# A fused attention and mixing kernel: first batch ordered by hand, constants moved to VectorE, later batches' reorder copies queued behind mixing, zero matmuls during the loads

## The chip, the cores and the metric

The kernel runs on one core of a Trainium2 chip. The metric is the device time of one execution in microseconds (us), the median of several executions on the chip. Single executions of the kernel before took 213.1 to 214.9 us. Runs are called fast or slow by their granted TensorE clock and time.

## The reference, cut to what matters

```python
B, H, S, D = 4, 8, 768, 64          # attention; then x is [4, 768, 512]
scores = q @ k.T / 8 + bias          # kept: 96 latest positions and 8 global ones
x = softmax(scores) @ v              # heads side by side
theta = x @ w_theta
zr, zi = x * cos(theta), x * sin(theta)
u = x + w_tok_r @ zr + w_tok_i @ zi  # over the 768 positions ("mixing")
out = u + relu(u @ w_ch)
```

The work is in bf16. For each batch: reorder and transpose q and k (four pairs of heads), scores, exponentials, values, transpose x, theta, mixing, the channel product.

## The kernel before: the parts that matter

The attention of batch b+1 is woven into the mixing of batch b, so that TensorE always has work. Batch 0 has no earlier batch and runs alone while the loads of everything else are still coming in. A scheduler decides the order of the instructions on each engine; the profile below shows what this means for VectorE, where a ready instruction stands behind a waiting one.

```python
def prep(b, p):                       # reorder a head pair (VectorE), transpose (TensorE)
    qkn = att.tile([T, NT, 2, 2, D], BF, name="qkn", bufs=3)
    for i_ in range(2):               # q, then k: each waits for its load
        nc.vector.tensor_copy(out=qkn[:, :, i_]..., in_=qk[:, i_, 2 * p:2 * p + 2])   # L175
    ...
        nc.tensor.transpose(ps[:, t_, :], qkn[:, t_, i_]..., ident)                    # L182

def values(b, p, hh): ...
    nc.vector.reciprocal(rec, po4[:, :, :, D:D + 1])                                   # L268
    nc.vector.tensor_mul(xv, po4[:, :, :, 0:D], rec...)      # x_sb, normalised          L270

def xtrans(b, p, copy): ...           # xT <- transposes of x_sb                         L275, L276

load_w(); load_all(1)
for p in range(NP):
    prep(0, p)
    for c in range(NT // 2):
        if p < NP - 1: scores(0, p, c)
globals_(0)
for p in range(NP):
    vglob(0, p); values(0, p, 0)
    if p < NT // 2: scores(0, NP - 1, p)
    values(0, p, 1)
    if p:
        trans_w(p - 1, nc.scalar.copy); xtrans(0, p - 1, nc.scalar.copy)
xtrans(0, NP - 1, nc.scalar.copy)
for b in range(B):                    # theta(b), then mixing woven with prep and attention of b+1
    ...
    pre = [(1536, lambda p=p: prep(nxt, p)) for p in range(NP)] if nxt else []
```

(Cuts are marked with "...".)

The softmax here doesn't subtract the row's maximum and nothing guards it: scores larger than these inputs give would overflow.

## Time and profile before

| | before |
|---|---|
| time, median of 3 | 213.73 us |
| span of the profile | 211.4 us |
| end of batch 0's last xT copy (theta can run in full) | 46.41 us |
| from there to the end | 164.96 us |

From the page of the kernel before: the busy tenths of TensorE and VectorE and the granted TensorE clock, in 40 slices of 5.3 us each.

```profile
PE   0586695388999999999999999999999999999971
DVE  3686352335698588657967667578666675652431
PEclk9999999579999999999999999999999999999997
```

TensorE (PE) is saturated from about 50 us on (nine tenths or more in every slice from 53 to 201 us). Before that it is not, and in the seventh and eighth slices (32 to 42 us) it is busy for only five and three tenths of the time. The VectorE (DVE) timeline around that point shows why. The columns are start, busy time, engine, source line, operation, output<-inputs; in brackets, the idle time before it and what ended it.

```profile
33.54 0.23 DVE L268 RECIPROCAL rec<-pb 128x12 f32<-128x12 f32 x1 [0.18 <-PE pb L264]
39.37 0.36 DVE L175 COPY qkn<-qk 128x768 bf16<-128x768 bf16 x1 [5.59 <-DMA qk<-in_q_dram]
39.64 0.95 DVE L270 TENSOR_TENSOR x_sb<-pb,rec 128x768 bf16<-128x768 f32 x1
40.51 0.62 DVE L175 COPY qkn<-qk 128x768 bf16<-128x768 bf16 x2
43.23 0.63 DVE L175 COPY qkn<-qk 128x768 bf16<-128x768 bf16 x2 [2.10 <-DMA qk<-in_k_dram]
43.77 0.23 DVE L268 RECIPROCAL rec<-pb 128x12 f32<-128x12 f32 x1
44.03 0.97 DVE L270 TENSOR_TENSOR x_sb<-pb,rec 128x768 bf16<-128x768 f32 x1
```

The reciprocal of pair 2 is done at 33.77 us and its multiplication could follow at once. Between the two stands a reorder copy of batch 1, which nobody needs yet and whose load lands at 39.37 us.

The TensorE timeline of the same kernel: six transposes of x_sb before 31 us, six of the weights after it, and the first instruction after the stall.

```profile
30.40 0.81 PE L275 MATMUL ps<-ident,x_sb 128*128 128x128 bf16 x6
31.11 0.50 PE L159 MATMUL ps<-ident,w_nat 128*128 128x128 bf16 x6
...
40.65 0.29 PE L275 MATMUL ps<-ident,x_sb 128*128 128x128 bf16 x1 [5.70 <-DVE x_sb L270]
```

Six transposes of the same shape take 0.81 us and then 0.50 us: from one to the next it is about 107 ns and then 55 ns. The array ran at half clock before 31 us: five transposes at 42.56 us, where the clock record has half clock, take 0.72 us, the same 107 ns from one to the next. The PEclk row shows a 9 there all the same (no clock record covers that time; the first begins at 31.06 us). TensorE then waits 5.70 us for the stalled multiplication.

### The profile page before, as it was taken

The numbers are of one execution on the slowest core, as the hardware profiler recorded it, in microseconds if no ns is written. First come the engines' busy times: TensorE is split into PE (matmuls) and PEld (weight loads), VectorE is DVE, ScalarE is ACT, GpSimd is POOL, SyncE is SP. The second block draws the span as 40 slices with busy tenths as digits, with TensorE's granted clock in tenths as the row PEclk, the third lists the DMA queues.
The fourth block names the chain that finished last, engine by engine and source line by source line (L and its number), as shares of the span: only waits on it lengthen the run. The fifth ranks groups of instructions, "written<-read, shape, count | busy, mean of one in ns | idle before, by whom it ended". The sixth has DMA issues, their size and how long they took to land.

```text
span 211.4 us, 4121 instructions
## 1 busy us (share of the span) xinstructions
PE 182.5 (86%) x1726; PEld 100.0 (47%) x1752; DVE 129.5 (61%) x268; ACT 119.4 (56%) x178; POOL 31.2 (15%) x46
## 2 busy tenths in 40 slices
PE   0586695388999999999999999999999999999971
PEld 0453484343464566645535555455354565344420
DVE  3686352335698588657967667578666675652431
ACT  2549859059459554269695652696956525912110
POOL 8992474040030000030000000000000000000000
PEclk9999999579999999999999999999999999999997
DMA  5999999999999611099011100110111011102121
GB/s 75 167 160 179 210 204 205 201 150 197 181 162 185 122 53 50 3 104 144 3 50 50 54 24 29 50 50 3 50 53 50 3 50 54 50 0 99 50 99 50
DMA packets 39329, 19.39 MB, mean 92 GB/s; under 512 B 25488, under 2 KB 36240, under 8 KB 39312
## 3 DMA queue, kind: packets, MB, share of 16 engines
q0 software_dynamic: 35856, 12.85, 61.5%
q1 hardware_dynamic: 3456, 6.29, 8.0%
q8 instruction: 13, 0.21, 0.4%
q14 instruction: 4, 0.03, 0.0%
HBM read 25.69 MB, written 6.29 MB: 151 GB/s over the span
## 4 chain that ended last, share of the span: by engine, by line
PE 66%; DMA 12%; DVE 9%; POOL 6%; issue 3%; ACT 2%; POOLq 0%; ACTq 0%
PE ps L305 28%; PE ps L325 10%; PE pb L290 7%; DMA qk<-in_k_dram 7%; PE pb L264 6%; DMA w_nat<-in_moe_w_tok_r_dram 5%; PE pb L222 4%; PE ps L316 3%; PE ps L182 3%; PE ps L275 2%; DVE zri L297 2%; POOL qk L72 2%; POOL vn L78 1%; DVE qT L187 1%; DVE o_sb L328 1%
## 5 line engine op out<-in xcount | busy, mean ns | idle before, releaser
L305 PE MATMUL ps<-zri,w_tokT_148 128*128 128x512 bf16 x141 | 53.2, 379 | 1.0 <-issue 0.2
L305 PE MATMUL ps<-zri,w_tokT_147 128*128 128x512 bf16 x128 | 48.4, 381 | 1.9 <-DVE zri L297 1.8
L318 ACT COPY uT<-ps 128x512 bf16<-128x512 bf16 x24 | 14.2, 590 | 37.0 <-PE ps L316 37.0
L328 DVE SCALAR_TENSOR_TENSOR o_sb<-ps,u 128x512 f32<-128x512 f32 x24 | 16.5, 689 | 25.4 <-PE ps L325 25.1
L325 PE MATMUL ps<-w_ch_bf,uT 128*128 128x512 bf16 x91 | 24.1, 380 | 1.2 <-ACT uT L318 0.7
L290 PE MATMUL pb<-w_theta_bf,xT 128*128 128x512 bf16 x94 | 24.2, 385 | 0.7 <-ACT xT L276 0.7
L182 PE MATMUL ps<-ident,qkn 128*128 128x128 bf16 x192 | 16.8, 242 | 8.5 <-DVE qkn L175 8.5
L305 PEld LDWEIGHTS <-w_tokT_147 128*128 128x128 bf16 x144 | 14.0, 97 | 16.0 <-issue 3.5
L297 DVE TENSOR_TENSOR zri<-x_sb,cs 128x1024 bf16<-128x1024 bf16 x24 | 16.2, 689 | 7.9 <-ACT cs L294 6.2
L222 PE MATMUL pb<-qT,kT 64*128 64x224 bf16 x192 | 18.4, 280 | 1.6 <-ACT e_110 L226 0.7
L182 PEld LDWEIGHTS <-qkn 128*128 128x128 bf16 x192 | 13.5, 108 | 12.8 <-DVE qkn L175 10.3
L305 PEld LDWEIGHTS <-w_tokT_148 128*128 128x128 bf16 x144 | 14.1, 98 | 11.5 <-DVE w_tokT_148 L160 0.3
L310 DVE TENSOR_TENSOR u<-x_sb,ps 128x512 bf16<-128x512 bf16 x24 | 16.4, 684 | 5.0 <-PE ps L305 5.0
L189 ACT COPY kT<-ps 128x768 bf16<-128x768 bf16 x16 | 12.7, 803 | 10.6 <-PE ps L182 10.3
L175 DVE COPY qkn<-qk 128x768 bf16<-128x768 bf16 x32 | 10.7, 376 | 11.4 <-DMA qk<-in_q_dram 8.1
L187 DVE COPY qT<-ps 128x768 bf16<-128x768 bf16 x16 | 15.2, 952 | 3.2 <-PE ps L182 3.1
L270 DVE TENSOR_TENSOR x_sb<-pb,rec 128x768 bf16<-128x768 f32 x16 | 15.3, 957 | 0.5
L78 POOL DMA_DIRECT2D vn<-in_v_dram x5 | 9.5, 1905 | 40.8 <-DVE rec L268 29.9
L290 PEld LDWEIGHTS <-xT 128*128 128x128 bf16 x96 | 8.9, 99 | 11.6 <-ACT xT L276 1.7
L275 PE MATMUL ps<-ident,x_sb 128*128 128x128 bf16 x96 | 9.0, 231 | 6.0 <-DVE x_sb L270 6.0
L222 PEld LDWEIGHTS <-kT 64*128 64x128 bf16 x192 | 6.8, 99 | 15.5 <-issue 12.9
L294 ACT ACTIVATE cs<-pb,halfpi 128x1024 bf16<-128x1024 f32 x12 | 13.4, 1114 | 1.3 <-PE pb L290 1.0
(116 smaller groups left out, 299.9 us busy)
## 6 DMA issues: line engine op xcount, KB each, us to landing
out_dram<-o_sb SPq DMA_DIRECT2D x24, 256.0 KB, 2.0
qk<-in_q_dram POOLq DMA_DIRECT2D x3, 768.0 KB, 11.9
qk<-in_k_dram POOLq DMA_DIRECT2D x3, 768.0 KB, 14.7
vn<-in_v_dram POOLq DMA_DIRECT2D x3, 768.0 KB, 17.8
w_nat<-in_moe_w_tok_r_dram POOLq DMA_DIRECT2D x6, 192.0 KB, 8.9
w_nat<-in_moe_w_tok_i_dram POOLq DMA_DIRECT2D x6, 192.0 KB, 8.5
qk<-in_q_dram POOLq DMA_DIRECT2D x4, 192.0 KB, 5.2
qk<-in_k_dram POOLq DMA_DIRECT2D x4, 192.0 KB, 5.3
```

The costliest lines, as they stand in the source:

```text
L182: nc.tensor.transpose(ps[:, t_, :], qkn[:, t_, i_].rearrange("p h d -> p (h d)"), ident)
L187: nc.vector.tensor_copy(out=dst, in_=src)
L222: nc.tensor.matmul(pb[:, hh, j * W:j * W + n], lhsT=kT[R, jt * T:(jt + 1) * T], rhs=qT[R, jt * T:jt * T + n], start=True, stop=True)
L270: nc.vector.tensor_mul(xv, po4[:, :, :, 0:D], rec.to_broadcast([T, 2, NT, D]))
L290: nc.tensor.matmul(pb[:, j, :], lhsT=xT[:, dc, st * T:(st + 1) * T], rhs=w_theta_bf[:, dc, :], start=(dc == 0), stop=(dc == NC - 1))
L294: nc.scalar.activation(cs[:, 0], pb, AF.Sin, bias=halfpi)
L297: nc.vector.tensor_mul(zri[b][:, i_, 2 * c:2 * c + 2, :], xb[:, 2 * c:2 * c + 2, :], cs[:, i_])
L305: nc.tensor.matmul(ps, lhsT=w_tokT[wi][:, st, tt * T:(tt + 1) * T], rhs=zri[b][:, wi, st, :], start=(st == 0 and wi == 0), stop=(st == NT ...
L310: nc.vector.tensor_add(u_sb[b, tt], x_sb[b][:, tt, :], ps)
L318: nc.scalar.copy(out=uT, in_=ps)
L325: nc.tensor.matmul(ps_c, lhsT=uT[:, dc, :], rhs=w_ch_bf[:, dc, :], start=(dc == 0), stop=(dc == NC - 1))
L328: nc.vector.scalar_tensor_tensor(o_sb, in0=ps_c, scalar=0.0, in1=u, op0=ALU.max, op1=ALU.add)
```

## The change

The intent: no load of a later batch may stall batch 0; TensorE in batch 0 gets a fixed order; the array is warmed by zero matmuls while loads land; GpSimd issues loads without constants in between. The diff, cut to its core:

```diff
-    load_qk(0, 0, 2)
-    make_identity(nc, ident, nomemset=True)        # GpSimd, between the loads
-    load_qk(0, 2, 2)
-    nc.gpsimd.iota(dist, ...) ; nc.gpsimd.affine_select(dist, ...)  (twice)
+    for p in range(NP):
+        load_qk(0, 2 * p, 2)
+    nc.vector.tensor_tensor_scan(ramp, ones, ones, -1.0, ...)
+    nc.vector.transpose(kmod, ramp[:, 0:GS])
+    ...                                            # pidx, ident, dist, grel: all on VectorE
+    zero = const.tile([T, 512], BF)
+    nc.vector.memset(zero, 0.0)
+    def warm(n):                                   # n zero matmuls, 512 columns
+    def behind(eng):
+        return tc.issue_after(anchor[eng]) if eng in anchor else nullcontext()
 def prep(b, p):
+        with behind("dve"):                        # queue behind the latest u of mixing
             nc.vector.tensor_copy(out=qkn[:, :, i_]..., in_=qk...)
+            with behind("pe"):                     # behind the latest mixing matmul
                 nc.tensor.transpose(ps[:, t_, :], qkn...)
 def mix(b, tt, g):
+                anchor["pe"] = nc.tensor.matmul(...).ins
+            anchor["dve"] = nc.vector.tensor_add(u_sb[b, tt], x_sb[b][:, tt, :], ps).ins
+    with tc.manual_schedule(engines={mybir.EngineType.PE}):
+        warm(8); prep(0, 0); warm(2)
+        for p in range(1, NP):
+            prep(0, p)
+            for c in range(NT // 2): scores(0, p - 1, c); warm(1)
+        globals_(0); vglob(0, 0..3)
+        for c in range(NT // 2): scores(0, NP - 1, c); warm(1)
+        for p in range(NP):
+            values(0, p, 0); values(0, p, 1)
+            if p: trans_w(p - 1, ...); xtrans(0, p - 1, ...)
+        trans_w(3, ...); xtrans(0, NP - 1, ...)
...
-        weave(main, pre + side, 0.15 if b == 0 else 0.0)
+        weave(main, pre + side, 0.3 if b == 0 else 0.0)
```

Smaller parts, not shown: the twelve loads of w_tok become six of double size; half of its transposes' copies go to VectorE; the fourth of six of these transposes moves from mixing into batch 0; batch 0's values are normalised head by head, in banks from the small PSUM pool.

More of the change, by code (lines that the diff above doesn't have):

```diff
@@ L1 @@
 import math
-from contextlib import ExitStack
+from contextlib import ExitStack, nullcontext
 import concourse.bass as bass
@@ L79, in load_v @@
                             in_=v[b, h0:h0 + n].rearrange("h (t p) d -> p (h t) d", p=T))
-    ident = const.tile([T, T], BF)
-    nc.gpsimd.memset(ident, 0.0)
     alloc_loads(0)
-    load_qk(0, 0, 2)
-    make_identity(nc, ident, nomemset=True)
-    load_qk(0, 2, 2)
-    dist = const.tile([T, W], FP)
-    nc.gpsimd.iota(dist, pattern=[[1, W]], base=0, channel_multiplier=-1,
-                   allow_small_or_imprecise_dtypes=True)
-    nc.gpsimd.affine_select(dist, dist, pattern=[[1, W]], base=0,
-                            channel_multiplier=-1, compare_op=ALU.is_ge, fill=1e6)
-    nc.gpsimd.affine_select(dist, dist, pattern=[[-1, W]], base=NL - 1,
-                            channel_multiplier=1, compare_op=ALU.is_ge, fill=1e6)
-    load_qk(0, 4, 2)
-    load_qk(0, 6, 2)
+    for p in range(NP):
+        load_qk(0, 2 * p, 2)
     load_v(0, 0, 4)
     load_v(0, 4, 4)
+    ones = const.tile([T, W], FP)
+    nc.vector.memset(ones, 1.0)
+    ramp = const.tile([T, W], FP)
+    nc.vector.tensor_tensor_scan(ramp, ones, ones, -1.0, op0=ALU.mult, op1=ALU.add)
+    kmod = const.tile([T, GS], FP)
+    nc.vector.transpose(kmod, ramp[:, 0:GS])
+    pidx = const.tile([T, 1], FP)
+    for p in range(NP):
+        nc.vector.tensor_scalar(pidx[GS * p:GS * (p + 1), :], kmod[GS * p:GS * (p + 1), 0:1],
+                                float(GS * p), None, op0=ALU.add)
+    ident = const.tile([T, T], BF)
+    nc.vector.tensor_scalar(ident, ramp[:, 0:T], pidx, None, op0=ALU.is_equal)
+    dist = const.tile([T, W], FP)
+    nc.vector.tensor_scalar(dist, ramp, pidx, None, op0=ALU.subtract)
+    far = const.tile([T, W], FP)
+    nc.vector.tensor_scalar(far, dist, 0.0, 1e6, op0=ALU.is_lt, op1=ALU.mult)
+    nc.vector.tensor_add(dist, dist, far)
+    nc.vector.tensor_scalar(far, dist, float(NL), 1e6, op0=ALU.is_ge, op1=ALU.mult)
+    nc.vector.tensor_add(dist, dist, far)
     etab = const.tile([T, H, W], BF)
@@ L115 @@
     grel = const.tile([T, T], FP)
-    for p in range(NP):
-        nc.gpsimd.iota(grel[GS * p:GS * (p + 1), :], pattern=[[1, T]], base=0, channel_multiplier=-1,
-                       allow_small_or_imprecise_dtypes=True)
+    nc.vector.tensor_scalar(grel, ramp[:, 0:T], kmod[:, 0:1], None, op0=ALU.subtract)
     gbias = const.tile([T, 2], FP)
@@ L148, in load_w @@
         nc.gpsimd.dma_start(out=w_theta_bf, in_=moe_w_theta.rearrange("(c p) n -> p c n", p=T))
-        for tt in range(NT):
+        for tt in range(0, NT, 2):
             for wi, src in enumerate((moe_w_tok_r, moe_w_tok_i)):
-                w_nat[wi, tt] = moe.tile([T, S], BF, name="w_nat", bufs=12)
-                nc.gpsimd.dma_start(out=w_nat[wi, tt], in_=src[tt * T:(tt + 1) * T, :])
+                w2 = moe.tile([T, 2, S], BF, name="w_nat", bufs=6)
+                nc.gpsimd.dma_start(
+                    out=w2, in_=src[tt * T:(tt + 2) * T, :].rearrange("(a p) s -> p a s", p=T))
+                w_nat[wi, tt], w_nat[wi, tt + 1] = w2[:, 0], w2[:, 1]
         nc.gpsimd.dma_start(out=w_ch_bf, in_=moe_w_ch.rearrange("(c p) n -> p c n", p=T))
@@ L159, in trans_w @@
                 nc.tensor.transpose(ps[:, st, :], w_nat[wi, tt][:, st * T:(st + 1) * T], ident)
-            copy(out=w_tokT[wi][:, :, tt * T:(tt + 1) * T], in_=ps)
+            (copy if wi else nc.vector.tensor_copy)(out=w_tokT[wi][:, :, tt * T:(tt + 1) * T], in_=ps)
+    zero = const.tile([T, 512], BF)
+    nc.vector.memset(zero, 0.0)
+    def warm(n):
+        ps = ps_small([T, 512], FP)
+        for _ in range(n):
+            nc.tensor.matmul(ps, lhsT=zero[:, 0:T], rhs=zero, start=True, stop=True)
     x_sb, xT_sb = {}, {}
@@ L165 @@
     egs = {}
+    anchor = {}
+    def behind(eng):
+        return tc.issue_after(anchor[eng]) if eng in anchor else nullcontext()
     def prep(b, p):
@@ L173, in prep @@
         qkn = att.tile([T, NT, 2, 2, D], BF, name="qkn", bufs=3)
-        for i_ in range(2):
-            nc.vector.tensor_copy(out=qkn[:, :, i_].rearrange("p t h d -> p h t d"),
-                                  in_=qk[:, i_, 2 * p:2 * p + 2])
+        with behind("dve"):
+            for i_ in range(2):
+                nc.vector.tensor_copy(out=qkn[:, :, i_].rearrange("p t h d -> p h t d"),
+                                      in_=qk[:, i_, 2 * p:2 * p + 2])
         qT = att.tile([T, S], BF, name="qT", bufs=6)
@@ L180, in prep @@
             ps = ps_small([T, NT, T], BF)
-            for t_ in range(NT):
-                nc.tensor.transpose(ps[:, t_, :], qkn[:, t_, i_].rearrange("p h d -> p (h d)"), ident)
+            with behind("pe"):
+                for t_ in range(NT):
+                    nc.tensor.transpose(ps[:, t_, :], qkn[:, t_, i_].rearrange("p h d -> p (h d)"), ident)
             dst = dst.rearrange("p (n t) -> p n t", t=NT)
@@ L253, in values @@
         vg = vgs[(b, p)]
-        if hh == 0:
-            pos[(b, p)] = ps_big()
-        po = pos[(b, p)]
+        if b == 0:
+            po = ps_small([T, 1, 512], FP)
+        else:
+            if hh == 0:
+                pos[(b, p)] = ps_big()
+            po = pos[(b, p)][:, hh:hh + 1, :]
         for it in range(NT):
@@ L261, in values @@
             mms.append((egs[b][hh][:, it * T:(it + 1) * T], vg[:, hh, :]))
-            o = po[:, hh, it * (D + 1):(it + 1) * (D + 1)]
+            o = po[:, 0, it * (D + 1):(it + 1) * (D + 1)]
             for i_, (l_, r_) in enumerate(mms):
                 nc.tensor.matmul(o, lhsT=l_, rhs=r_, start=(i_ == 0), stop=(i_ == len(mms) - 1))
-        if hh == 1:
-            po4 = po[:, :, 0:NT * (D + 1)].rearrange("p a (t d) -> p a t d", d=D + 1)
-            rec = att.tile([T, 2, NT, 1], FP, name="rec")
-            nc.vector.reciprocal(rec, po4[:, :, :, D:D + 1])
-            xv = x_sb[b][:, :, p * T:(p + 1) * T].rearrange("p t (a d) -> p a t d", a=2)
-            nc.vector.tensor_mul(xv, po4[:, :, :, 0:D], rec.to_broadcast([T, 2, NT, D]))
+        if b and hh == 0:
+            return
+        if b:
+            po = pos[(b, p)]
+        h0, n = (2 * p + hh, 1) if b == 0 else (2 * p, 2)
+        po4 = po[:, :, 0:NT * (D + 1)].rearrange("p a (t d) -> p a t d", d=D + 1)
+        rec = att.tile([T, n, NT, 1], FP, name="rec", tag=f"rec{n}")
+        nc.vector.reciprocal(rec, po4[:, :, :, D:D + 1])
+        xv = x_sb[b][:, :, h0 * D:(h0 + n) * D].rearrange("p t (a d) -> p a t d", a=n)
+        nc.vector.tensor_mul(xv, po4[:, :, :, 0:D], rec.to_broadcast([T, n, NT, D]))
     def xtrans(b, p, copy=nc.vector.tensor_copy):
@@ L304, in mix @@
             for wi in range(2):
-                nc.tensor.matmul(ps, lhsT=w_tokT[wi][:, st, tt * T:(tt + 1) * T],
-                                 rhs=zri[b][:, wi, st, :], start=(st == 0 and wi == 0),
-                                 stop=(st == NT - 1 and wi == 1))
+                anchor["pe"] = nc.tensor.matmul(
+                    ps, lhsT=w_tokT[wi][:, st, tt * T:(tt + 1) * T], rhs=zri[b][:, wi, st, :],
+                    start=(st == 0 and wi == 0), stop=(st == NT - 1 and wi == 1)).ins
         if g == NT // 2 - 1:
             u_sb[b, tt] = moe.tile([T, DM], BF, name="u", bufs=4)
-            nc.vector.tensor_add(u_sb[b, tt], x_sb[b][:, tt, :], ps)
+            anchor["dve"] = nc.vector.tensor_add(u_sb[b, tt], x_sb[b][:, tt, :], ps).ins
     def utrans(b, tt):
@@ L377 @@
     load_all(1)
-    for p in range(NP):
-        prep(0, p)
-        for c in range(NT // 2):
-            if p < NP - 1:
-                scores(0, p, c)
-    globals_(0)
-    for p in range(NP):
-        vglob(0, p)
-        values(0, p, 0)
-        if p < NT // 2:
-            scores(0, NP - 1, p)
-        values(0, p, 1)
-        if p:
-            trans_w(p - 1, nc.scalar.copy)
-            xtrans(0, p - 1, nc.scalar.copy)
-    xtrans(0, NP - 1, nc.scalar.copy)
+    with tc.manual_schedule(engines={mybir.EngineType.PE}):
+        warm(8)
+        prep(0, 0)
+        warm(2)
+        for p in range(1, NP):
+            prep(0, p)
+            for c in range(NT // 2):
+                scores(0, p - 1, c)
+                warm(1)
+        globals_(0)
+        for p in range(NP):
+            vglob(0, p)
+        for c in range(NT // 2):
+            scores(0, NP - 1, c)
+            warm(1)
+        for p in range(NP):
+            values(0, p, 0)
+            values(0, p, 1)
+            if p:
+                trans_w(p - 1, nc.scalar.copy)
+                xtrans(0, p - 1, nc.scalar.copy)
+        trans_w(3, nc.scalar.copy)
+        xtrans(0, NP - 1, nc.scalar.copy)
     tail = []
@@ L405 @@
             for g in range(NT // 2):
-                if g == 0 and b == 0 and tt >= NP - 1:
-                    main.append((1536, lambda tt=tt: trans_w(tt)))
                 main.append((2048, lambda tt=tt, g=g: mix(b, tt, g)))
+                if b == 0 and g == 1 and tt < 2:
+                    main.append((1536, lambda tt=tt: trans_w(tt + 4)))
                 if tt and g == 0:
```

## The prediction

> **What bounds the kernel now.** From 50 us on, TensorE is the limit: the table of stretches gives it 9.5 to 10.0 busy of every 10 us from 70 to 200 us. The first 50 us are different.
>
> 1. A stall by queue order. In the timeline, pair 2's normalisation (reciprocal done at 33.77 us) sits on VectorE behind a reorder copy of the *next* batch, which waits 5.59 us for its q load (39.37). TensorE then idles 5.70 us (34.95 to 40.65). A second copy waits 2.10 us for the k load (43.23) ahead of pair 3's reciprocal. The last xT copy ends at 46.41 us. [...]
> 2. A cold array. The page shows full clock before 31 us, but in the timeline six transposes take 0.82 us until 30.4 and 0.49 after 31.1; 65-column matmuls step by 55 ns at 25 to 30 us and by 30 at 32.5. It is cold again from 40.7 to 44. [...] this trace warms after about 5 us of dense value matmuls.
> 3. ScalarE does about 30 us of work before theta, with waits between; pair 3's exponentials run only at 27 to 33 us.
>
> **What the change does.** Later batches' reorder copies queue behind mixing: the 5.59 and 2.10 us waits leave VectorE's queue (about 6.5 us of chain). The hand order puts all scores first, then values. Zero matmuls (22 at 0.22 warm to 0.43 us cold) should warm the array early: values and transposes then take about half. Half of the early weight transposes' copies move from ScalarE (0.86 us) to VectorE (0.55). A third of the later ones (12 x 57 ns = 0.7 us) leaves mixing. Constants move from GpSimd (about 3 us between load issues) to VectorE (about 20 small operations, estimated 4 us at the 0.2 to 0.3 us of its existing ones): loads are issued 1 to 2 us earlier, but DMA moves 160 to 205 GB/s from 5 us on, so they land about 1 us earlier.
>
> **Sum.** First exponential near 11 us as now (11.40); ScalarE then has about 17 us up to pair 3's exponentials (about 28); the value phase overlaps their end and needs about 9 us on TensorE, VectorE and ScalarE alike. Last xT copy at about 37 us instead of 46.4: 9 us. Minus 0.7 us of transposes, give or take 1 us for batch 1's changed weaving: 213.7 - 9.5 = **204.2 us**, range 200.8 to 208.6. Faster by over 2%: 0.93; within 2%: 0.06; slower: 0.01.
>
> **What would show it.** VectorE's waits for batch 1's loads between 33 and 43 us gone; no TensorE idle stretch over 3 us after 10 us; transposes at about 57 ns from about 10 us; first Sin activation at 37 to 40 us (47.75 now); last xT copy to the end as long as before (about 161 us). Most of the gain should be the stall, 2 to 3 us the warm array, under 1 us the constants.
>
> **What would make it wrong.** Constants delaying the first reorder copies or the zeros on VectorE, so the fixed order starts late and zeros hold up the first transposes; the array not staying warm; four small PSUM buffers serialising the value phase; mixing, starting earlier, catching up with batch 1's loads (DMA is busy until 68 us), which moves the stall rather than removes it.

Two passages are cut from this text and marked. Neither is a term of the sum, which stays 213.7 - 9.5 = 204.2 us.

## More of the kernel before

A profile shows one single execution: for the kernel before one of 213.15 us, for the changed kernel one of 204.92 us, the slowest of its set of four. Its span is 1.8 to 2.3 us shorter than the time measured for it.

## The result, and the profile after

Ratios are the mean time of one kernel's fast runs over the mean of the kernel before's of the same rounds, so not quite the ratio of the medians quoted.

| | before | after |
|---|---|---|
| time, median | 213.79 us | 204.32 us |
| ratio, 95% interval | | 0.956 (0.953 to 0.959) |
| span of the profile | 211.4 us | 203.1 us |
| end of batch 0's last xT copy | 46.41 us | 38.18 us |
| from there to the end | 164.96 us | 164.96 us |

All of the 8.2 us by which the two profiles differ came from the start. (The medians differ by 9.5 us; the profiled execution of the change was the slowest of its set.) The page after, the same three rows:

```profile
PE   0599799989799999998999999989999999999972
DVE  7988578176964788779656778688377675642431
PEclk9999969999999999999999999999999999999996
```

The hole in the seventh and eighth slices is gone. One slice of reduced clock is left, at 25 to 30 us. (The clock at the start is again not recorded.) The VectorE timeline after, where the stall had been:

```profile
31.75 0.20 DVE L300 RECIPROCAL rec<-ps 128x6 f32<-128x6 f32 x1 [0.32 <-PE ps L292]
31.98 0.56 DVE L302 TENSOR_TENSOR x_sb<-ps,rec 128x384 bf16<-128x384 f32 x1
...
51.85 0.89 DVE L199 COPY qkn<-qk 128x768 bf16<-128x768 bf16 x3
```

The multiplication follows its reciprocal at once, and the reorder copies of batch 1 come at 51.85 us without a wait. The start of the same run, though, shows two new things:

```profile
6.82 0.27 DVE L140 MEMSET shift<- 128x256 uint32 x1
7.10 0.27 DVE L172 MEMSET zero<- 128x256 uint32 x1
7.43 3.59 PE L177 MATMUL ps<-zero 128*128 128x512 bf16 x8 [7.43 <-DVE zero L172]
7.57 1.12 DVE L199 COPY qkn<-qk 128x768 bf16<-128x768 bf16 x1
10.81 1.36 PE L207 MATMUL ps<-ident,qkn 128*128 128x128 bf16 x12
...
14.01 1.73 ACT L251 ACTIVATE e_115<-pb 128x896 bf16<-128x896 f32 x2
```

VectorE makes constants until past 7 us, so the first reorder copy starts at 7.57 us (4.85 before) and the zero tile is late. The eight zero matmuls then hold TensorE until about 11 us, with the first transposes behind them. The first exponential on ScalarE (ACT) runs at 14.01 us; before it was 11.40. So the start got later, and still its end came 8 us earlier. The experiments sort this out.

Because all stages between two theta phases look alike, a good ruler for the rest is the start of ScalarE's table load for Sin, once per batch:

| | batch 0 ready | batch 0 to 1 | 1 to 2 | 2 to 3 | 3 to end |
|---|---|---|---|---|---|
| before | 46.42 | 45.60 | 42.46 | 42.64 | 34.25 |
| after | 38.19 | 45.43 | 42.71 | 42.94 | 33.87 |

### The profile page after: what moved, and what is told of

Read it like the earlier page. It is cut to its first block, busy times and chain, and to the rows that moved or that the text cites. A ratio compares the mean times of both kernels' runs of the same rounds, so it can differ in the third digit from the quotient of the medians.

```text
span 203.1 us, 4198 instructions
## 1 busy us (share of the span) xinstructions
PE 183.0 (90%) x1774; PEld 97.9 (48%) x1774; DVE 136.9 (67%) x293; ACT 117.8 (58%) x176; POOL 26.7 (13%) x31
## 4 chain that ended last, share of the span: by engine, by line
PE 80%; ACT 10%; DVE 8%; issue 1%; ACTq 0%
PE ps L337 31%; PE ps L357 11%; PE pb L322 8%; PE pb L292 7%; PE ps L207 5%; PE pb L247 5%; PE ps L348 3%; PE ps L307 3%; PE ps L292 3%; PE ps L177 2%; PE ps L167 2%; DVE o_sb L360 1%; DVE u L342 1%; DVE zri L329 1%; ACT kT L214 1%
## 5 line engine op out<-in xcount | busy, mean ns | idle before, releaser
L337 PE MATMUL ps<-zri,w_tokT_151 128*128 128x512 bf16 x144 | 54.5, 380 | 1.8 <-DVE zri L329 1.8
L337 PE MATMUL ps<-zri,w_tokT_152 128*128 128x512 bf16 x144 | 54.3, 379 | 0.0
L357 PE MATMUL ps<-w_ch_bf,uT 128*128 128x512 bf16 x96 | 24.9, 380 | 0.8 <-ACT uT L350 0.7
L247 PE MATMUL pb<-qT,kT 64*128 64x224 bf16 x192 | 17.4, 256 | 1.8 <-ACT e_117 L251 0.5
L177 PE MATMUL ps<-zero 128*128 128x512 bf16 x22 | 9.1, 486 | 8.0 <-DVE zero L172 7.4
L207 PE MATMUL ps<-ident,qkn 128*128 128x128 bf16 x192 | 14.1, 224 | 2.2 <-DVE qkn L199 2.2
L207 PEld LDWEIGHTS <-qkn 128*128 128x128 bf16 x192 | 12.3, 101 | 6.0 <-DVE qkn L199 3.5
L357 PEld LDWEIGHTS <-uT 128*128 128x128 bf16 x96 | 7.9, 97 | 9.9 <-ACT uT L350 2.9
L327 ACT ACTIVATE cs<-pb 128x1024 bf16<-128x1024 f32 x12 | 12.2, 1020 | 0.0
```

The lines of the kernel that those rows point to most:

```text
L207: nc.tensor.transpose(ps[:, t_, :], qkn[:, t_, i_].rearrange("p h d -> p (h d)"), ident)
L247: nc.tensor.matmul(pb[:, hh, j * W:j * W + n], lhsT=kT[R, jt * T:(jt + 1) * T], rhs=qT[R, jt * T:jt * T + n], start=True, stop=True)
L337: anchor["pe"] = nc.tensor.matmul(ps, lhsT=w_tokT[wi][:, st, tt * T:(tt + 1) * T], rhs=zri[b][:, wi, st, :], start=(st == 0 and wi == 0), ...
L357: nc.tensor.matmul(ps_c, lhsT=uT[:, dc, :], rhs=w_ch_bf[:, dc, :], start=(dc == 0), stop=(dc == NC - 1))
```

## The experiments

All times are medians; "before" of the same rounds was 213.5 to 213.9 us throughout. The changed kernel itself was repeated on the chip of the first three runs.

> The changed kernel itself, on the same chip as the three others, so that differences of 0.5 per cent can be read: 204.3 us within 0.5.

Measured: 204.62 us, ratio 0.958 (0.956 to 0.960). It agrees with the first measurement.

### 1. The queueing alone

```diff
 # kernel before, plus behind(), anchor["dve"] and anchor["pe"] as in the change; nothing else
```

> The kernel before, with one part of the change: later batches' reorder copies (VectorE) and their transposes (TensorE) queued behind the mixing. Theory A (the queue-order stall is nearly all of the 8 us that the start lost): pair 2's normalisation follows its reciprocal at 33.8 us, the last xT copy ends at 38 to 40 us instead of 46.4, time 205 to 207.5 us. Rival B (the stall was one link among several, and hand order, warm array and constants bring as much): last xT copy at 42 us or later, time 209 to 211 us.

Measured: 206.26 us, ratio 0.966 (0.965 to 0.967). The last xT copy ends at 38.73 us:

```profile
37.93 0.80 ACT L282 COPY xT<-ps 128x768 bf16<-128x768 bf16 x1 [0.82 <-PE ps L281]
```

This one part brings 7.25 us (213.51 - 206.26) of the 8.9 that the whole change brings in the same rounds (213.51 - 204.62). Theory A holds. With TensorE's idle stretch the lost clock went as well: in the kernel before the record has half clock from 37.89 to 44.72 us, and in this run it has full clock from 28.29 to 202.37 us. What part of the 7.25 us that makes was not measured apart.

### 2. The change without the queueing

```diff
-        return tc.issue_after(anchor[eng]) if eng in anchor else nullcontext()
+        return nullcontext()
```

> The changed kernel with only the queueing behind mixing taken out. Its VectorE program then has three reorder copies of batch 1 ahead of pair 3's table products, so it stands until about 38 us for a load. Theory A: the stall returns, larger than before since the whole value phase follows it; last xT copy near 48 to 50 us, time 212 to 217 us. Rival B: hand order and warm array keep half or more of the gain, time 207 to 209 us.

Measured: 219.71 us, ratio 1.029 (1.027 to 1.031), slower than the kernel before and above the expected range. VectorE in this run:

```profile
24.59 0.22 DVE L229 TENSOR_TENSOR eg<-eg,gmask 128x128 bf16<-128x128 bf16 x1 [0.57 <-ACT eg L228]
40.03 0.90 DVE L199 COPY qkn<-qk 128x768 bf16<-128x768 bf16 x3 [15.21 <-DMA qk<-in_q_dram]
```

VectorE stands for 15.21 us behind the same load, from 24.8 us on (5.59 us in the kernel before, from 33.8 on). Batch 0 had got faster, so VectorE arrived at that copy earlier and waited longer; and with a fixed TensorE order everything queues behind it: TensorE waits 16.0 us in one piece. Runs 1 and 2 together show the cause from both sides.

### 3. The change without zero matmuls

```diff
-        warm(8) ... warm(2) ... warm(1)     # all 22
```

> The changed kernel without its 22 zero matmuls. My prediction gave the warm array 2 to 3 us: then 206.3 to 207.3 us. Rival, from the changed kernel's trace: the first eight zeros hold TensorE from 7.43 to 11.02 us while the first reorder copies are done near 8.0 us, ScalarE's exponentials limit the time from 13 to 25 us, and the array was cold again at 25.5 to 29 us, so the zeros give nothing net: first transposes near 8.3 us, first exponential near 12.5 instead of 14.0, value phase about 1 us slower, time 203.3 to 204.8 us.

Measured: 204.52 us, ratio 0.958 (0.956 to 0.961), as the changed kernel's 204.62. The zeros give nothing measurable. Two traces show the balance. Without zeros the first exponential is at 12.76 us instead of 14.01. With zeros the scores run at full clock (clock 1.00 from 11.9 to 25.5 us; four score matmuls take 0.37 us, without zeros 0.48; twelve transposes 0.83 us, without 1.46), but ScalarE's exponentials set the pace there (ScalarE is busy 5.00 of 5 us from 15 to 20 and from 20 to 25 us after the change). Both kernels end pair 3's last exponential at nearly the same time, 27.1 and 27.3 us. And in the profiled execution the clock has just been lost again when the dense value matmuls come. The changed kernel in stretches of 3.4 us (columns: stretch, length, busy time and count of each engine, granted clock, DMA, GB/s):

```profile
18.70:22.10 3.40, 2.77 (x32) 1.40 (x33) 2.87 (x6) 3.40 (x7) 1.00 (x2) 1.00 1.21 211
22.10:25.50 3.40, 2.46 (x30) 0.89 (x22) 1.33 (x5) 3.40 (x10) 1.53 (x2) 1.00 1.15 206
25.50:28.90 3.40, 3.23 (x49) 2.68 (x49) 2.26 (x7) 1.64 (x4) 2.58 (x2) 0.51 1.16 209
```

After a stretch in which TensorE was busy 2.46 of 3.40 us the granted clock halves for exactly one stretch, 3.41 us in the clock record (25.57 to 28.98 us), the one with the first value matmuls. No wait of TensorE between 12 and 25.5 us was over 0.6 us. The busy share alone does not decide this: in the same trace TensorE was busy 2.35 of 3.40 us from 49.50 to 52.90 us and kept the full clock; in run 5's trace the clock was kept after 2.03 us (9.34 to 12.76). What does decide it is not shown. At the start, zeros run from 7.43 us on and full clock is recorded from 11.9 us, 4.5 us later. That time is not the same in every execution: the eight zeros take 3.59 us here and 3.60 in the last kernel, but 3.19 in run 5, which has the same program as the last kernel up to there; so in run 5 the pace rose before they ended.

The stretch is not lost in every execution. The profiles of behind_b1 and behind_theta (experiment 7) have the same instructions in the first batch, and there the clock stays full (1.00 from 0 to 38 us): from the end of pair 3's last exponential to batch 0 being ready they take 10.03 us each, against 11.06 and 11.05 us in the two profiles of the change, which both lost it, and 11.21 without zeros. A kept clock is thus worth about 1 us there. Five of the nine executions of the change have a mean granted clock of 0.993 or more, which leaves no room for a half stretch of 3.41 us (estimated at 0.5 x 3.41 / 203.1 = 0.0084 of the mean). They took 203.7 to 204.6 us; the kernel without zeros took 203.9 to 205.2. So even then the gain is not clear of the spread, and the lost clock is not the whole reason; what else cancels it stays open.

### 4. The zeros made first

```diff
+    zero = const.tile([T, 512], BF)
+    nc.vector.memset(zero, 0.0)
     alloc_loads(0)
```

> The changed kernel with the zero tile filled first on VectorE, so that the eight zero matmuls run at about 1.5 to 5 us instead of 7.43 to 11.02 and no longer stand ahead of the first transposes. Theory C (the zeros' place costs what their warmth brings): first transposes near 8.2 us, first exponential near 12 us (14.0 in the changed kernel, 12.8 without zeros), time 202.5 to 203.8 us. Rival D (the start of the exponentials is not what the value phase waits for): 204.1 to 204.9 us as with and without zeros.

Measured: 204.73 us over six runs, of which one is slow (219.86 us at a granted clock of 0.833); the five fast ones have the median 204.68 us and the ratio 0.955 (0.953 to 0.958). That is not distinguishable from the changed kernel and in rival D's range, so theory C fell: taking the zeros out of the transposes' way, by itself, wins nothing measurable. The profile fell in the slow run and is not read for times, so how much earlier the exponentials start in a fast execution is not shown.

### 5. The constants back on GpSimd

```diff
-    ones, ramp, kmod, pidx, ident, dist, grel on VectorE
+    ident, dist and grel on GpSimd between the loads, as before
```

> The changed kernel with the constants made on GpSimd between the loads, as before. The prediction gave the move of the constants to VectorE under 1 us of gain: then 204.6 to 205.6 us. Rival, from the changed kernel's trace: its VectorE makes constants until 7.3 us while the first loads have landed near 5 to 6 us, so the move costs; with constants on GpSimd the first transposes start after the zeros near 7 us instead of 10.8 and the time is 202.5 to 204.2 us.

Measured: 202.97 us, ratio 0.950 (0.947 to 0.953); a second run, described below, gave 202.89. This is faster than the change. The first reorder copies of this run (VectorE timeline) against 7.57 us in the changed kernel:

```profile
4.89 0.36 DVE L193 COPY qkn<-qk 128x768 bf16<-128x768 bf16 x1 [1.45 <-DMA qk<-in_q_dram]
6.29 0.54 DVE L193 COPY qkn<-qk 128x768 bf16<-128x768 bf16 x1 [1.04 <-DMA qk<-in_k_dram]
```

VectorE now waits for the loads, as it should. The first exponential comes at 11.06 us, and batch 0 is ready at 35.5 us instead of 38.2 to 38.5. Moving the constants to VectorE therefore cost about 1.5 us of time (0.957, the middle of the two ratios of the changed kernel, minus 0.950, of 213.7 us). The profiles differ by more, 2.7 and 3.0 us, because both of the changed kernel are the slowest executions of their sets (204.92 and 205.32 us). The edit also moves the first zeros forward, from 7.43 to 3.28 us; by run 4 that alone gains nothing. The prediction had booked a gain of under 1 us. Part of the delay may be the copies themselves: the first takes 1.12 us in the changed kernel and 0.36 here, and in the changed kernel GpSimd is issuing the v loads at that time (7.04 to 9.99 us). But the copy at 4.89 us in this run also ran while GpSimd issued a load (4.89 to 5.61 us) and took 0.36, so overlap alone does not explain the 1.12 us, and no run here isolates its cause.

### 6. The scheduler's order instead of the hand's

```diff
-    with tc.manual_schedule(engines={mybir.EngineType.PE}):
+    with nullcontext():
```

> The changed kernel traced in the same order, but with TensorE's order in the first batch left to the scheduler. With one part alone giving 7.3 of 8.9 us, the hand order can be worth at most about 1.5 us: 204.0 to 206.0 us; above 206 the hand order would matter more than I now think.

Measured: 204.18 us, ratio 0.956 (0.954 to 0.959). Fixing TensorE's order gives nothing measurable once the other parts are in place. The statements are still traced in the new order here; only the fixing is taken away.

### 7. Where the queueing itself costs: other places for the anchor

In the mixing stages of the changed kernel TensorE waits for the reorder copies, which wait for a sum u of mixing. The waits of TensorE from 38 us to the end, after the change:

```profile
PE ps L207 <- DVE qkn L199: 2.2, 3, 1.1
PE ps L337 <- DVE zri L329: 1.8, 4, 0.9
```

(Columns: total, times, longest, in us.) Before, the copies cost TensorE 0.2 us there. The first try queued batch 1 only, on VectorE only, behind the last theta product:

```diff
-        with behind("dve"):
+        with behind("dve") if b == 1 else nullcontext():
...
+                anchor["dve"] = nc.vector.tensor_mul(zri[b]..., xb..., cs[:, i_]).ins   # theta
```

> The changed kernel with the queueing kept for batch 1 alone, on VectorE alone, and behind the last product of theta instead of the latest mixing sum. In the changed kernel TensorE waits 1.05, 0.57 and 0.57 us for the reorder copies of batches 1, 2 and 3 (0.21 in all before). Theory E: these 2.2 us are the price of queueing behind a sum that itself waits for mixing; they go, time 202.0 to 203.0 us. Rival F: TensorE loses them elsewhere (VectorE is busy 7 to 9 of 10 us there): 203.8 to 204.8 us.

Measured: 208.08 us, ratio 0.973 (0.971 to 0.975). Neither theory had this. The stall came back one batch later:

```profile
57.90 0.36 DVE L199 COPY qkn<-qk 128x768 bf16<-128x768 bf16 x1 [3.37 <-DMA qk<-in_k_dram]
```

This is batch 2's copy, free to move now, which the scheduler put in the middle of batch 1's work. Its load lands at 57.9 us. TensorE lost 3.6 us and then the clock (mean granted clock 0.95 from 38 to 60 us and 0.92 from 60 to 90; 1.00 in both for the repeated change). The second try gave every later batch the theta anchor:

> The changed kernel with every later batch's reorder copies queued behind the last product of the running batch's theta instead of behind its latest mixing sum, and the transposes not queued at all. Theory E: the anchor on the mixing sum makes TensorE wait 2.2 us in three mixing stages; with the earlier anchor these waits go, and the stall does not return because batch 2's copies stay out of batch 1's stage (the failure of the run that queued batch 1 alone): 202.0 to 203.0 us. Rival F: VectorE gives the time back elsewhere: 203.8 to 204.8 us.

Measured: 206.71 us, ratio 0.968 (0.966 to 0.971), 2 us slower than the change: theory E fell for the whole, and the ruler shows where. Batch 0 to 1 took 44.20 us (45.43), so that stage shrank as expected, but 1 to 2 took 44.36 (42.71) and 2 to 3 took 44.60 (42.94). The VectorE timelines of batch 1's theta tell why. After the change:

```profile
83.15 1.16 DVE L199 COPY qkn<-qk 128x768 bf16<-128x768 bf16 x4
86.16 1.51 DVE L329 TENSOR_TENSOR zri<-x_sb,cs 128x1024 bf16<-128x1024 bf16 x2
```

With the theta anchor:

```profile
84.14 1.50 DVE L329 TENSOR_TENSOR zri<-x_sb,cs 128x1024 bf16<-128x1024 bf16 x2
...
89.70 1.42 DVE L199 COPY qkn<-qk 128x768 bf16<-128x768 bf16 x5
```

For the first four of the eight copies of batches 2 and 3 the latest mixing sum, at the place where the copy is traced, is one of the batch that came before the running one: the change's anchor is the earlier of the two there. These four copies run ahead of the theta products, 0.5 us before the Sin table load, and their transposes fill TensorE while it would wait for those products. Behind the theta anchor they come 8.1 us after that load, and TensorE waits for theta products 3.7 us in all instead of 1.8. These 1.9 us are part of the 3.3 us by which the two stages grew; the rest is not traced to a wait. This run also takes the queueing off the transposes. The same anchor in the kernel before:

> The kernel before, with its reorder copies queued behind the last theta product, and nothing else of the change. If the stall is nearly all and the anchor's place costs about 2 us, this one ordering constraint does as much as the whole change: 204.0 to 205.2 us (206.3 with the anchor on the mixing sum).

Measured: 209.49 us, ratio 0.980 (0.978 to 0.982): outside the expectation too, with the same lengthening, 44.41 and 44.60 us. This kernel differs from the kernel before (42.46 and 42.64) by the anchor of the copies alone, so the anchor is the cause. Its start is as good as in run 1 (Sin table load at 38.82 us), so the loss is again in the later stages. So the change's queueing (copies and transposes together) costs 1.2 us in batch 1's stage (45.43 against 44.20; in the kernel before the two anchors differ by only 0.1 us there, 45.78 in run 1 against 45.68), and in the two later ones 0.25 and 0.30 us against the kernel before (42.71 and 42.94 against 42.46 and 42.64); the 2.2 us of waits were not all there to be had.

The kernel of run 5 again, without the new anchor:

> A second look at the changed kernel with constants on GpSimd (mislabelled: the kernel submitted is the one without the new anchor): 202.2 to 203.8 us as before.

Measured: 202.89 us in one run. It serves as a repeat of run 5, with batch 0 ready at 35.63 us (35.53).

### 8. Put together

```diff
 # run 5 (constants on GpSimd), and in prep:
-        with behind("dve"):
+        with behind("th" if b == 1 else "dve"):          # "th": last theta product
-            with behind("pe"):
+            with behind("pe") if b > 1 else nullcontext():
```

> Two findings put together: the changed kernel with constants on GpSimd (202.9 us, the stages from theta on unchanged), and with batch 1's copies alone queued behind the last theta product, batches 2 and 3 as in the change. From one Sin table load to the next, batch 1's stage took 44.2 us with that anchor and 45.4 with the change's, while batches 2 and 3 took 44.4 to 44.6 with it and 42.7 to 42.9 with the change's. If these add: 202.9 - 1.2 = 201.7, between 201.2 and 202.4 us. If they don't add, 202.6 to 203.3.

Measured: 202.16 us, ratio 0.944 (0.940 to 0.948), the fastest and clearly better than both kernels given. Against run 5 (0.950, 0.947 to 0.953) the intervals overlap, so that step is not proven by time. In the trace, batch 1's stage is 44.20 us as hoped; but batch 0 was ready at 36.74 us in that execution instead of 35.5, with the same program up to there: its eight zeros took 3.60 us instead of 3.19, and six transposes of pair 1 waited 0.76 us for their copy. The clock record differs too: half clock for 6.83 us (21.51 to 28.33) instead of the 3.41 us of run 5's profile (23.00 to 26.41), and from pair 3's last exponential to batch 0 being ready it took 11.77 us instead of 11.12. The spans of the two profiles are equal, 200.5 us.

## Why the prediction was right

The time was right: 204.2 us predicted, 204.32 and 204.62 measured. Point by point the account is less even: that the sum came out this close is partly luck, since errors cancelled.

- The stall: right in cause and size. The prediction took 6.5 us of chain for it. Queueing alone brought 7.25 us, and taking queueing away made the change 15 us slower.
- "2 to 3 us the warm array": wrong, the zeros gave nothing measurable. The array did warm (full clock recorded from 11.9 us), but that phase is paced by ScalarE, and in both profiles of the change the clock is lost just when the value matmuls need it. Where it was kept, that phase was about 1 us shorter.
- "under 1 us the constants": wrong in sign, a loss of about 1.5 us. The prediction costed them at 4 us of VectorE and named the danger, that they delay the first reorder copies; it then set the first exponential at 11 us "as now". It came at 14.0. That is the step that failed.
- "12 x 57 ns = 0.7 us leaves mixing": the transposes left, but batch 1's stage shrank by only 0.17 us (45.60 to 45.43), at least in part because TensorE now waits 1.05 us there for a copy queued behind a mixing sum.
- The last xT copy: 38.2 us instead of 37, pair 3's exponentials ended at 27.1 us (28 predicted), the longest TensorE wait after 10 us was 1.05 us (under 3 predicted). The prediction's "about 161 us from the last xT copy to the end" was misread, since it left off at the last matmul: it is 164.96 us, before and after alike, so the statement that it stays the same held.
- Between queueing alone (206.3) and the whole change (204.6) lie 1.7 us net, although constants cost 1.5. The other parts together bring about 3 us: run 5, the change without the moved constants, is 3.3 us faster than queueing alone (202.97 against 206.26), and its batch 0 is ready 3.2 us earlier (35.53 against 38.75). Hand order and zeros each bring nothing measurable when taken out alone, so what is left is the other order of statements, values normalised head by head, paired w_tok loads, copies shared between two engines, the moved transposes and the later weaving. Which of these it is stays open. The traces only show that pair 3's last exponential ends at 24.4 us in run 5 and at 32.5 us in run 1.

## What to carry to other kernels

On VectorE a ready instruction behind one that waited for a load cost the whole wait here (5.59 us in the kernel before, 15.21 in run 2); look in the timeline for a short operation on the critical chain directly after a long "DMA" wait, and queue early-prefetch work behind the point where its data is sure to be there. Where it is queued matters too: too late made the consumer wait (TensorE 1.05 us in batch 1's stage), not at all brought the stall back (15.21 us in run 2), and for batch 1 alone brought it back one batch later (3.37 us). Before moving work off an engine, read what the receiving engine does first in that stage, and test warm-up tricks against a version without them.
